# A next chunk's first matmuls issued two steps ahead, and one small copy moved from GpSimd to VectorE

## The chip, the core and the metric

The kernel runs on one core of a Trainium2 chip. The metric is the time of one execution on the device in microseconds (us), lower is better. The engines are called by their short names: PE (TensorE, matmuls), DVE (VectorE), ACT (ScalarE), POOL (GpSimd) and SP (SyncE, which here only issues DMAs). Each engine works through its own instructions in order; ACT, POOL and SP also issue DMAs from their queues.

## The reference

The input x has 2048 rows and 1024 columns (S and D), the hidden width F is 3584. Cut to what matters:

```python
xn = layernorm(x)                                  # over the 1024 columns
X  = rfft2(xn) * (w_r + 1j * w_i)                  # 2048 x 513
s  = irfft2(X, s=(2048, 1024))
h  = silu(xn @ w1)                                 # 2048 x 3584
g  = silu(h @ w2)                                  # 2048 x 1024
return x + s * g
```

So there are two branches on the same normalised input: a two-dimensional Fourier filter, and a feed-forward block. All is float32 in and out.

## The kernel before, in words

Every float32 matmul operand is split into a high and a low float16 part, and each product is made of three passes (high by high, high by low, low by high). The split of a weight is one ACT instruction (the high part, a function `high`, L257) and one DVE instruction (the low part, `low`, L260).

The rows are cut into four chunks c = 0 to 3 of 512 rows, each of four tiles p of 128 rows. `xnT[c]` holds a chunk's normalised input, transposed and split.

PE's stream is a row of groups of the feed-forward block, with the pieces of the Fourier branch set in between:

- First layer, `pa(c,f)` (L466): 24 matmuls of 512 columns for chunk c and the f-th of 28 slices of 128 hidden columns. ACT evacuates a group with silu into `h`; four PSUM buffers (tag "ff") are shared by these groups and a few small sums. After four groups DVE and ACT form sums and differences of h (`hr`, `hosum`, `hoone`), split them, and SP stores them (the `hd` tensors).
- Second layer, `pb(m,j)` (L549 to L551): seven products m, Strassen's way, of eight blocks j. Its weights are loaded by SP as `jr`, for the products m = 4 and 5 joined with a second block by an accumulating DMA that POOL issues (L424), and split by ACT and DVE into `w`. DVE adds the results up in `kept` and `pl`.

The Fourier branch has three stages, each a Python generator that emits its instructions step by step:

- Forward, `fd_gen(c)`: for each tile p the transform over d by 24 matmuls of 128 columns (`fa_mat`, PE L803 to L805, tile `fa(c,p)`), evacuated by two ACT instructions (`fa_evac`, L812 and L813) into `L0`, of which there are two buffers. DVE then does butterflies over each tile (`bfly`), writing `V`. After the four tiles, four steps j = 0 to 3 do a radix-4 step on DVE over the tiles, split the result (`Rs`, ACT L884 and L886, DVE L889 and L890), and SP stores it (`vd`, `vs`).
- Filter, `f_gen`: sixteen tiles `fx(u)`, matmuls over the rows with loaded constants `kq` and the stored `vq`, then on DVE butterflies, the multiplication with w (loaded as `wq`), butterflies back, a split `zq` and a store `zd`. The values at column 512 go another way, through small tensors `zp` and `zps`.
- Inverse, `i_gen(c)`, in the order c = 1, 3, 0, 2: `load_i` loads `zt` from `zd`, `edge_in` copies the column from `zps` (odd c) or `zp` (even c) into `zt` (128 partitions x 16 elements), then four tiles `iu` (PE L1281 for odd c, L1289 for even c), each evacuated by ACT (`uc`) and DVE (`ub`, L1297 and L1298), and four tiles `id` after them.

The tiles `fa`, `fx`, `iu` and `id` all take turns in two PSUM buffers (tag "ft"), so a tile's matmuls wait until the tile two before it has been evacuated.

The order of all this is written by the kernel itself, at build time. After each group of pa or pb a function `work` takes one step of the weight queue, one of an auxiliary queue, and up to three steps of the background queue that holds the Fourier generators. It stops as soon as a modelled DVE clock is more than 1.0 us ahead of a modelled PE clock, or when a step yields PAUSE. The clocks are advanced by every DVE and PE instruction emitted, by a fixed cost and one per element; the numbers that other steps yield play no part. A step can correct the DVE clock by hand, as the four radix-4 steps do with `clock["dve"] -= 0.8`. So how much background work stands between two pa groups follows from these numbers; on the chip the engines then run through their queues in that order, whatever it costs.

In the forward stage, the steps i = 0 to 5 of a chunk issue fa(c,i) in step i, evacuate fa(c,i−1) and do the butterflies of tile i−2. For chunk 0 the matmuls and the first two evacuations are emitted elsewhere, ahead of the generator.

Of the kernel before, what the change touches and what calls it, by code (L numbers as in the profile page):

```python
# [26 lines left out]
IORDER = (1, 3, 0, 2)  # L27
# [105 lines left out]
def spectral_ffn(ctx, tc, x, w_r, w_i, w1, w2, ca, kc, ci, tw, pm, out):  # L133
    nc = tc.nc
# [35 lines left out]
    zps = cp.tile([128, 2, 4, 4, 2], F16, name="zps")  # L170
# [45 lines left out]
    clock = {"pe": 0.0, "dve": 0.0}  # L216
# [16 lines left out]
    def radix4(sign, b, d, o):  # L233

        sub = nc.vector.tensor_tensor
        plus, minus = ((2, 7), (6, 3)) if sign < 0 else ((6, 3), (2, 7))

        def pick(i):
            st = i[1] - i[0]
            stop = i[1] + (1 if st > 0 else -1)  # L240
            return o[:, i[0]:stop:st]

        sw = d[:, 1, ::-1]
        sub(o[:, 0:2], b[:, 0], b[:, 1], op=OP.add)
        sub(o[:, 4:6], b[:, 0], b[:, 1], op=OP.subtract)
        sub(pick(plus), d[:, 0], sw, op=OP.add)
        sub(pick(minus), d[:, 0], sw, op=OP.subtract)
# [551 lines left out]
    def fa_mat(c, p):  # L799
        ps = pt.tile([128, 8, 128], F32, name=f"fa{c}_{p}", tag="ft")  # L800
        sl, xt = slice(p * 128, (p + 1) * 128), xnT[c]
        for d in range(8):
            nc.tensor.matmul(ps[:, d], xt[:, 0, d, sl], A["ca"][:, 0, d], start=True, stop=False)  # L803
            nc.tensor.matmul(ps[:, d], xt[:, 0, d, sl], A["ca"][:, 1, d], start=False, stop=False)
            nc.tensor.matmul(ps[:, d], xt[:, 1, d, sl], A["ca"][:, 0, d], start=False, stop=True)  # L805
        psa[c, p] = ps

    def fa_evac(c, p):
        ps = psa.pop((c, p))
        t0 = A["p"].tile([128, 8, 2, 65], F32, name=f"L0_{c}_{p}", tag="L0", bufs=2)  # L810
        nc.gpsimd.memset(t0[:, :, 1, 0:1], 0.0)
        nc.scalar.activation(t0[:, :, 0], ps[:, :, 0:65], AF.Copy)  # L812
        nc.scalar.activation(t0[:, :, 1, 1:64], ps[:, :, 65:128], AF.Copy)  # L813
        l0[c, p] = t0

    def fd_gen(c):
# [51 lines left out]
            tt(v[:, 1, 0:1], ee[:, 0, 0, 0:1], ee[:, 1, 0, 0:1], op=OP.subtract)  # L868

        for i in range(6):  # L870
            if i < 4 and c:
                fa_mat(c, i)
            if 1 <= i <= 4 and (c or i > 2):
                fa_evac(c, i - 1)
            yield 0
            if i >= 2:
                yield from bfly(i - 2)
            yield 0
        o, sp, total, both = {}, {}, {}, {}

        def high_r(j):
            room = ap.tile([128, 2048 + 256 * len(THREE)], F16, name=f"Rs{c}_{j}", tag="Rs", bufs=2)
            both[j] = room[:, 2048:].rearrange("p (q h k) -> p q h k", h=2, k=128)
            nc.scalar.activation(both[j][:, :, 0], total[j], AF.Copy, scale=2.0**-21)  # L884
            sp[j] = room[:, 0:2048].rearrange("p (q h k) -> p q h k", h=2, k=256)
            nc.scalar.activation(sp[j][:, :, 0], o[j], AF.Copy, scale=2.0**-21)  # L886

        def low_r(j):
            nc.vector.scalar_tensor_tensor(sp[j][:, :, 1], o[j], 2.0**-21, sp[j][:, :, 0], op0=OP.mult, op1=OP.subtract)  # L889
            nc.vector.scalar_tensor_tensor(both[j][:, :, 1], total[j], 2.0**-21, both[j][:, :, 0], op0=OP.mult, op1=OP.subtract)  # L890
            defer(2, lambda: nc.sync.dma_start(vd[j][:, :, c], sp[j]))
            defer(2, lambda: nc.sync.dma_start(vs[j][:, :, c], both[j]))

        for j in range(4):
            sl = slice(128 * j, 128 * j + 128)
            if j:
                high_r(j - 1)
            b = ap.tile([128, 2, 2, 128], F32, name=f"Rb{c}_{j}", tag="Rb", bufs=1)
            d = ap.tile([128, 2, 2, 128], F32, name=f"Rd{c}_{j}", tag="Rd", bufs=1)
            nc.vector.tensor_tensor(b, vt[:, 0:2, :, sl], vt[:, 2:4, :, sl], op=OP.add)  # L900
            nc.vector.tensor_tensor(d, vt[:, 0:2, :, sl], vt[:, 2:4, :, sl], op=OP.subtract)
            if j:
                low_r(j - 1)
            r = ap.tile([128, 8, 128], F32, name=f"Ro{c}_{j}", tag="Ro", bufs=1)
            radix4(-1, b, d, r)
            o[j] = r.rearrange("a (q r) k -> a q (r k)", r=2)
            total[j] = ap.tile([128, len(THREE), 128], F32, name=f"vt{c}_{j}", tag="E", bufs=1)
            some = o[j][:, THREE[0]:THREE[-1] + 1]
            nc.vector.tensor_tensor(total[j], some[:, :, 0:128], some[:, :, 128:256], op=OP.add)
            clock["dve"] -= 0.8  # L910
            yield 3.9
        high_r(3)
        yield 0.5
# [332 lines left out]
    def edge_in(c):  # L1246
        zt = C["z"][c]
        if c % 2:
            zt = zt.rearrange("m (e q h l i) -> m e q h l i", e=2, q=4, h=2, l=8)
            nc.gpsimd.tensor_copy(zt[:, :, :, :, 0, 0], zps[:, :, c])  # L1250
        else:
            zt = zt.rearrange("m (q h r l i) -> m q h r l i", q=4, h=2, r=2, l=8)
            nc.gpsimd.tensor_copy(zt[:, :, :, :, 0, 0], zp[:, c].rearrange("m r q h -> m q h r"))

    def i_gen(c):
        ip = C["p"]
        tt, stt = nc.vector.tensor_tensor, nc.vector.scalar_tensor_tensor
        if c == IORDER[0]:
            edge_in(c)
# [187 lines left out]
        for p in range(5):  # L1447
            if p < 4:
                mat2(p)
            if p:  # L1450
                bfly(p - 1)
            if p == 3 and c != IORDER[-1]:
                edge_in(IORDER[IORDER.index(c) + 1])
            yield 3.4 if p else 0.3
# [41 lines left out]
    with tc.manual_schedule():  # L1496
# [73 lines left out]
        for c in range(4):  # L1570
            add(bg, fd_gen(c))
# [140 lines left out]
```

## Time and profile before

| what | us |
|---|---|
| median of 3 runs (lowest 1228.38, highest 1229.40) | 1229.09 |
| the profiled execution | 1229.27 |
| its span, first to last instruction | 1227.5 |
| PE busy | 1211.4 |
| DVE busy | 1003.7 |
| ACT busy | 496.1 |
| POOL busy | 140.2 |

The granted clock of PE is full (1.00) throughout. By time, the first layer with the forward stage takes the first 635 us, the filter runs from 552 to 839, the second layer from 635 on, the inverse from 879. A row of a timeline reads: start, duration, engine, line, operation, output and input tiles with shapes, count, and in brackets how long the engine had been idle before it and which instruction ended that. A row of the list of waits reads: the waiting engine and its line, the engine it waited for, total us, how many times, the longest.

### The profile page before, as it was taken

Reading aid. Unit: us, or ns where it says so; the run is one execution under the profiler, and the core shown is the slowest. Engines: PE = TensorE matmul, PEld = TensorE weight load, DVE = VectorE, ACT = ScalarE, POOL = GpSimd, SP = SyncE. Lnnn points to the kernel's source line nnn. Section 1 sums busy time; section 2 is a strip of 40 time slices with the busy share of each in tenths; the row PEclk is TensorE's granted clock in tenths of the full one; section 3 lists DMA queues with packets and bytes.
Section 4 is the critical chain, followed back from the end, with each engine's and each line's share of the span. In section 5 each row is a group of like instructions: output and inputs, shape, how many; then the busy total and the mean of one; then the engine's idle time right before and its main releaser. Section 6 shows DMA issues by size and latency. Waiting matters only on the chain.

```text
span 1227.5 us, 19143 instructions
## 1 busy us (share of the span) xinstructions
PE 1211.4 (99%) x6992; PEld 615.1 (50%) x6992; DVE 1003.7 (82%) x2006; ACT 496.1 (40%) x670; POOL 140.2 (11%) x256
## 2 busy tenths in 40 slices
PE   8999999999999999999999999999999999999998
PEld 5544445445444544445445555554445554455545
DVE  7778997898798798958969989995377876997766
ACT  6775553455375654434423222221122322333212
POOL 3320100002010000201101121152111111000000
PEclk9999999999999999999999999999999999999999
DMA  8887585747678978489998999977979999996677
GB/s 251 184 195 188 165 255 180 211 130 214 192 254 276 317 231 270 146 259 208 188 282 279 263 253 233 315 255 221 269 218 302 264 338 310 305 364 244 224 249 274
DMA packets 285055, 299.98 MB, mean 244 GB/s; under 512 B 48928, under 2 KB 211744, under 8 KB 284576
## 3 DMA queue, kind: packets, MB, share of 16 engines
q1 hardware_dynamic: 264944, 239.95, 66.9%
q10 hardware_dynamic: 15840, 50.67, 11.8%
q0 software_dynamic: 4176, 8.13, 3.6%
q8 instruction: 55, 0.90, 0.3%
q14 instruction: 40, 0.33, 0.1%
HBM read 188.05 MB, written 104.35 MB: 238 GB/s over the span
## 4 chain that ended last, share of the span: by engine, by line
PE 59%; DMA 15%; DVE 14%; ACT 3%; issue 3%; SPq 1%; POOL 1%; ACTq 0%; DVEq 0%; POOLq 0%
PE pa L466 33%; PE pb L551 7%; PE pb L549 7%; PE pb L550 7%; DMA jr<-in_B_w_dram 2%; PE id L1371 2%; DMA jr<-ws 1%; DVE Z L1124 1%; DVE w L260 1%; DMA cis<-in_ci_dram 1%; DMA ht<-hd_dif 1%; ACT xp L750 1%; DMA vq<-vd 1%; DMA zd<-zq 1%; DMA zt<-zd 1%
## 5 line engine op out<-in xcount | busy, mean ns | idle before, releaser
L466 PE MATMUL pa<-xnT,w 128*128 128x512 f16 x2688 | 584.3, 379 | 1.3 <-ACT w L257 0.7
L466 PEld LDWEIGHTS <-w 128*128 128x128 f16 x2688 | 261.2, 98 | 312.7 <-issue 1.2
L549 PE MATMUL pb<-w,ht 128*128 128x512 f16 (+2 forms) x812 | 300.4, 372 | 0.0
L550 PE MATMUL pb<-w,ht 128*128 128x512 f16 (+2 forms) x812 | 300.4, 372 | 0.0
L551 PE MATMUL pb<-w,ht 128*128 128x512 f16 (+2 forms) x812 | 300.3, 372 | 0.0
L551 PEld LDWEIGHTS <-ht 128*128 128x128 f16 x812 | 79.4, 98 | 91.1
L549 PEld LDWEIGHTS <-ht 128*128 128x128 f16 x812 | 79.5, 98 | 86.7
L550 PEld LDWEIGHTS <-ht 128*128 128x128 f16 x812 | 79.4, 98 | 86.8
L475 ACT ACTIVATE h<-pa,s 128x512 f32<-128x512 f32 x112 | 75.6, 677 | 77.6 <-PE pa L466 60.2
L257 ACT ACTIVATE w<-jr,sc 128x512 f16<-128x512 f32 x98 | 68.4, 713 | 86.4 <-DMA jr<-in_B_w_dram 45.6
L260 DVE SCALAR_TENSOR_TENSOR w<-jr,sc,w 128x512 f16<-128x512 f32 x98 | 71.3, 743 | 18.8 <-ACT w L257 18.8
L257 ACT ACTIVATE hosum<-hr,hs 128x1536 f16<-128x1536 f32 x28 | 44.0, 1573 | 87.5 <-DVE hr L505 34.9
L260 DVE SCALAR_TENSOR_TENSOR hoone<-h,hs,hoone 128x2048 f16<-128x2048 f32 x28 | 65.6, 2342 | 7.2 <-ACT hoone L257 7.2
L257 ACT ACTIVATE hoone<-h,hs 128x2048 f16<-128x2048 f32 x28 | 55.9, 1995 | 28.6 <-issue 11.1
L504 DVE TENSOR_TENSOR hr<-h 128x1024 f32<-128x1024 f32 x28 | 34.1, 1219 | 21.8 <-ACT h L475 21.8
L260 DVE SCALAR_TENSOR_TENSOR hosum<-hr,hs,hosum 128x1536 f16<-128x1536 f32 x28 | 50.7, 1810 | 1.4 <-ACT hosum L257 1.4
L257 ACT ACTIVATE w<-w1r,rs 128x1024 f16<-128x1024 f32 x28 | 31.9, 1143 | 37.7 <-DVE w L260 24.2
L642 ACT ACTIVATE pl<-pl,c 128x512 f32<-128x512 f32 (+2 forms) x28 | 17.7, 656 | 70.2 <-DVE pl L618 43.6
L424 POOL DMA_DIRECT2D jr<-in_B_w_dram x28 | 24.6, 999 | 180.3 <-DMA jr<-in_B_w_dram 89.7
L1124 POOL TENSOR_TENSOR Z<-yb 128x32 f32<-128x32 f32 x32 | 16.2, 525 | 209.0 <-DVE yb L1103 202.2
L1033 ACT ACTIVATE zq<-Z,zs 128x1024 f16<-128x1024 f32 x16 | 18.4, 1148 | 52.5 <-DVE Z L1124 25.6
L260 DVE SCALAR_TENSOR_TENSOR w<-w1r,rs,w 128x1024 f16<-128x1024 f32 x28 | 35.6, 1273 | 2.3 <-ACT w L257 2.2
(239 smaller groups left out, 1571.6 us busy)
## 6 DMA issues: line engine op xcount, KB each, us to landing
w1r<-in_B_w_dram SPq DMA_DIRECT2D x28, 512.0 KB, 6.6
hd_sum<-hosum SPq DMA_DIRECT2D x56, 256.0 KB, 2.9
hd_one<-hoone SPq DMA_DIRECT2D x56, 256.0 KB, 4.0
hd_dif<-hoone SPq DMA_DIRECT2D x56, 256.0 KB, 4.3
w2m<-in_B_w_dram SPq DMA_DIRECT2D x28, 512.0 KB, 5.6
ht<-hd_dif ACTq DMA_DIRECT2D x32, 448.0 KB, 9.2
jr<-in_B_w_dram SPq DMA_DIRECT2D x56, 256.0 KB, 6.7
ht<-hd_sum ACTq DMA_DIRECT2D x32, 448.0 KB, 5.7
```

What stands on the lines that cost most here:

```text
L257: nc.scalar.activation(hi, raw, AF.Copy, scale=scale)
L260: nc.vector.scalar_tensor_tensor(lo, raw, scale, hi, op0=OP.mult, op1=OP.subtract)
L424: nc.gpsimd.dma_start(raw[n], w2_block(*todo[n], 1), accum_op=OP.add)
L466: nc.tensor.matmul(ps, w[:, wh, d], xt[:, xh, d], start=(n == 0), stop=(n == 23))
L475: nc.scalar.activation(hq[:, 2 * (c % 2) + f % 2], ps, AF.Silu, scale=s1[:, f:f + 1])
L504: tt(sums[:, 0:2], hq[:, 0::2], hq[:, 1::2], op=OP.subtract)
L549: nc.tensor.matmul(ps, hh[:, 0], w[:, 0], start=first, stop=False)
L550: nc.tensor.matmul(ps, hh[:, 0], w[:, 1], start=False, stop=False)
L551: nc.tensor.matmul(ps, hh[:, 1], w[:, 0], start=False, stop=last)
L1033: nc.scalar.activation(zqs[q][:, 0, :, 16 * j:16 * j + 16], zs_[u], AF.Copy, scale=zs)
L1124: eng.tensor_tensor(Z[:, ns, pos], x0[:, :, ls], x1[:, :, ls], op=o_)
L1371: nc.tensor.matmul(ps[:, g, cols], us[g][:, uh, 4 * r + p], C["ci"][:, ch, g, r, cols], start=(r == 0 and n == 0), stop=(r == 1 and n == 2 ...
```

## The change

It has three parts.

First, the matmuls of a chunk's first two tiles in the transform over d, fa(c,0) and fa(c,1), and the evacuation of fa(c,0), are emitted in the radix-4 steps j = 2 and 3 of the chunk before. Within the chunk, step i = 0 issues fa(c,2) and evacuates fa(c,1), step i = 3 issues fa(c,3) and evacuates fa(c,2), step i = 4 evacuates fa(c,3). So each tile's matmuls come two steps ahead of its butterflies. Chunk 0 stays as it was.

Second, the hand correction of the modelled DVE clock in a radix-4 step is 0.5 instead of 0.8.

Third, the copy into zt for the inverse's first chunk (c = 1) is a DVE instruction; for the three others it stays on POOL.

```diff
         for i in range(6):
-            if i < 4 and c:
-                fa_mat(c, i)
-            if 1 <= i <= 4 and (c or i > 2):
-                fa_evac(c, i - 1)
+            if i in (0, 3) and c:
+                fa_mat(c, 2 + i // 3)
+            if i in (0, 3, 4) and (c or i):
+                fa_evac(c, max(i, 2) - 1)
             yield 0
...
         for j in range(4):
+            if j > 1 and c < 3:
+                fa_mat(c + 1, j - 2)
+                if j > 2:
+                    fa_evac(c + 1, 0)
...
-            clock["dve"] -= 0.8
+            clock["dve"] -= 0.5
             yield 3.9
...
         if c % 2:
             zt = zt.rearrange("m (e q h l i) -> m e q h l i", e=2, q=4, h=2, l=8)
-            nc.gpsimd.tensor_copy(zt[:, :, :, :, 0, 0], zps[:, :, c])
+            (nc.vector if c == IORDER[0] else nc.gpsimd).tensor_copy(zt[:, :, :, :, 0, 0], zps[:, :, c])
```

From here on lines of the changed kernel stand four higher than the same lines before, from L900 on. Three places show what moves. Tile names in these rows carry chunk and number, then a running number that means nothing.

ACT around the evacuations of fa(3,0) and fa(3,1), before (`h32` is h, `w2m` a running maximum over w2, `w1` a weight split):

```order
L475 ACTIVATE h32_8_1_4109<-pa2_17_4081,s1_229 128x512
L257 ACTIVATE w1_21_4185<-w1r21_3823,rs1_228 128x1024
L390 ACTIVATE junk_248,w2m_232<-w2m14_3977 128x1024
L812 ACTIVATE L0_3_0_4219<-fa3_0_4126 128x8x65
L813 ACTIVATE L0_3_0_4219<-fa3_0_4126 128x8x63
L475 ACTIVATE h32_8_1_4109<-pa3_16_4151,s1_229 128x512
L390 ACTIVATE junk_248,w2m_232<-w2m15_4016 128x1024
L812 ACTIVATE L0_3_1_4292<-fa3_1_4194 128x8x65
L813 ACTIVATE L0_3_1_4292<-fa3_1_4194 128x8x63
```

Here the evacuation of fa(3,0) stands behind a weight split. The same engine now:

```order
L475 ACTIVATE h32_8_0_3916<-pa0_17_3888,s1_229 128x512
L390 ACTIVATE junk_248,w2m_232<-w2m11_3841 128x1024
L812 ACTIVATE L0_3_0_4032<-fa3_0_3927 128x8x65
L813 ACTIVATE L0_3_0_4032<-fa3_0_3927 128x8x63
L884 ACTIVATE Rs2_2_4036<-vt2_2_3966 128x2x128
L886 ACTIVATE Rs2_2_4036<-Ro2_2_3961 128x4x256
L475 ACTIVATE h32_8_0_3916<-pa1_16_3968,s1_229 128x512
L390 ACTIVATE junk_248,w2m_232<-w2m12_3883 128x1024
L884 ACTIVATE Rs2_3_4093<-vt2_3_4050 128x2x128
L886 ACTIVATE Rs2_3_4093<-Ro2_3_4045 128x4x256
L475 ACTIVATE h32_8_0_3916<-pa1_17_4052,s1_229 128x512
L812 ACTIVATE L0_3_1_4168<-fa3_1_4007 128x8x65
```

The two evacuations come four and three pa groups earlier, among the last steps of chunk 2 (Rs2). On PE the sequence of whole groups was pa(2,17), fa(3,0), pa(3,16), fa(3,1), pa(3,17), fa(3,2), and is now pa(0,17), fa(3,0), pa(1,16), fa(3,1), pa(1,17), pa(2,16), fa(3,2).

The copy into zt for chunk 1, before, on POOL (`jr` are second-layer weights, the DMA rows their joins):

```order
L424 DMA jr56_8644<-in_B_w2_dram 128x512
L424 DMA jr57_8675<-in_B_w2_dram 128x512
L424 DMA jr58_8701<-in_B_w2_dram 128x512
L1250 COPY zt1_8581<-zps_220 128x16
L424 DMA jr59_8733<-in_B_w2_dram 128x512
```

Here the copy stands behind the joins jr56 to jr58. DVE around the same place now:

```order
L598 TENSOR_TENSOR kept5_7103<-kept5_7103,pb2_5_8652 128x512
L260 SCALAR_TENSOR_TENSOR w2_3_1_8544<-jr54_8572,sc2_234,w2_3_1_8544 128x512
L260 SCALAR_TENSOR_TENSOR w2_3_1_8544<-jr55_8619,sc2_234,w2_3_1_8544 128x512
L1254 COPY zt1_8581<-zps_220 128x16
L598 TENSOR_TENSOR kept6_7180<-kept6_7180,pb2_6_8710 128x512
L1301 TENSOR_TENSOR ub1_0_8840<-iu1_0_8788,uc1_0_8838 128x512
```

It leaves the queue of the joins and stands between the split of jr55 and the addition of pb(2,6). The other rows of DVE around it are in the order they had.

SP around the last store of the forward stage (`vd3`, `vs3`) and the first load of the filter (`vq0`), before:

```order
L498 DMA hd_one_0_1_99<-hoone_0_10_1_5226 512x1x256
L498 DMA hd_dif_1_1_91<-hoone_0_10_1_5226 512x1x256
L498 DMA hd_dif_0_1_93<-hoone_0_10_1_5226 512x1x256
L498 DMA hd_one_3_1_97<-hoone_0_10_1_5226 512x1x256
L891 DMA vd3_78<-Rs3_3_5233 512x1x512
L892 DMA vs3_82<-Rs3_3_5233 256x1x256
L966 DMA vq0_5356<-vd0_75 128x2048
```

Here vd3 and vs3 stand behind the four stores of hoone. SP at the same place now:

```order
L891 DMA vd3_78<-Rs3_3_5235 512x1x512
L892 DMA vs3_82<-Rs3_3_5235 256x1x256
L498 DMA hd_one_0_1_99<-hoone_0_10_1_5226 512x1x256
L498 DMA hd_dif_1_1_91<-hoone_0_10_1_5226 512x1x256
L498 DMA hd_dif_0_1_93<-hoone_0_10_1_5226 512x1x256
L498 DMA hd_one_3_1_97<-hoone_0_10_1_5226 512x1x256
L970 DMA vq0_5321<-vd0_75 128x2048
```

The two stores of the forward stage pass the four stores of hoone. The loads vq0 and kq0 wait for vs3 to land, before and now. On PE the first filter tile fx0 stood after pa(0,27) and stands after pa(0,26); from the sixth filter tile on, and through the inverse, PE's order is what it was.

## The prediction

> **What bounds the kernel now.** I read the page's busy times, then the waits of PE, then the timelines of the engines around the two waits that the change touches, and last the windows of DMA share.
>
> ```profile
> span 1227.5 us, 19143 instructions
> PE 1211.4 (99%) x6992; PEld 615.1 (50%) x6992; DVE 1003.7 (82%) x2006; ACT 496.1 (40%) x670; POOL 140.2 (11%) x256
> ```
>
> PE is busy for all but 16.1 us of the span, and the change takes no matmul away, so it can only win what PE waits. These are PE's waits, without those of the first 20 us:
>
> ```profile
> PE iu L1281 <- POOL zt L1250: 2.6, 1, 2.6
> PE iu L1289 <- DVE ub L1298: 1.8, 1, 1.8
> PE fa L803 <- ACT L L813: 1.3, 1, 1.3
> ...
> PE pa L466 <- DMA xnT<-xs: 0.6, 1, 0.6
> ```
>
> Each is one single wait. The change aims at the first (the copy into the inverse's first tile) and the third (a tile of the transform over d). It does not touch the code of the other two.
>
> **The wait of fa.** PE around it, then ACT:
>
> ```profile
> 407.90 5.34 PE L466 MATMUL pa<-xnT,w 128*128 128x512 f16 x24
> 414.58 0.22 PE L803 MATMUL fa<-cas,xnT 128*128 128x128 f16 x1 [1.34 <-ACT L L813]
> ```
>
> ```profile
> 411.37 1.15 ACT L257 ACTIVATE w<-w1r,rs 128x1024 f16<-128x1024 f32 x1 [2.14 <-DVE w L260]
> 412.43 1.04 ACT L390 ACTIVATE junk<-w2m 128x1024 fp8e4<-128x1024 f32 x1
> ...
> 413.95 0.58 ACT L813 ACTIVATE L<-fa 128x504 f32<-128x504 f32 x1
> ```
>
> This is fa(3,2): two PSUM buffers are shared by the fa tiles, so it needs the evacuation of fa(3,0), and that evacuation stands in ACT's queue behind a weight split, which itself waited for DVE until 411.37. Between fa(3,0) and fa(3,2) stand two groups of 24 pa matmuls. In the new order there are three (pa of (1,16), (1,17) and (2,16)), each worth the row below, and the evacuation stands right behind the h of pa(0,17), ahead of the splits of Rs.
>
> ```profile
> 189.99 5.18 PE pa L466 x24
> ```
>
> So the evacuation gets 5.18 us more against a lateness of 1.34: this term is −1.34 us; it begins to shrink only if ACT were 3.84 us later there than now, and is gone at 5.18. For chunks 1 and 2 the same tiles have three groups or more, and no wait stands there today. The 48 matmuls and two evacuations moved per chunk for chunks 1 to 3 keep their number and size, so on PE they cost 0. On ACT an evacuation now comes up to four groups earlier; what could suffer is the evacuation of a pa tile behind it, but four pa buffers give three groups (15.5 us), and the list of PE's waits holds no pa that waited for an evacuation. I take 0, with −1.34 and +1.34 as the ends for a wait of the same size that goes or comes elsewhere. The constant 0.8 that becomes 0.5 adds no instruction; it lets the planner hand out less background work per matmul group: 0 by itself.
>
> **The copy into the inverse's first tile.** PE, POOL, DVE and ACT around it:
>
> ```profile
> 876.73 0.38 PE L551 MATMUL pb<-w,ht 128*128 128x512 f16 x1
> 879.72 2.85 PE L1281 MATMUL iu<-kk,zt 128*128 128x128 f16 x48 [2.61 <-POOL zt L1250]
> ```
>
> ```profile
> 876.66 2.74 POOL L424 DMA_DIRECT2D jr<-in_B_w_dram  x3 [41.31 <-DMA jr<-in_B_w_dram]
> 878.41 1.26 POOL L1250 COPY zt<-zps 128x16 f16<-128x16 f16 x1
> ```
>
> ```profile
> 876.12 0.75 DVE L260 SCALAR_TENSOR_TENSOR w<-jr,sc,w 128x512 f16<-128x512 f32 x1 [11.22 <-ACT w L257]
> 876.79 0.68 DVE L598 TENSOR_TENSOR kept<-kept,pb 128x512 f32<-128x512 f32 x1
> 881.90 0.69 DVE L1297 TENSOR_TENSOR ub<-iu,uc 128x512 f32<-128x512 f32 x1 [4.43 <-ACT uc L1295]
> ```
>
> On POOL the copy stands behind three DMA issues (the joins of jr56 to jr58) that wait for loads, and it takes 1.26 us. On DVE it stands behind the split of jr55 and ahead of kept, so it can start where kept started, at 876.79. No row shows this copy on DVE. The nearest is a DVE instruction of 32 elements:
>
> ```profile
> L1209 DVE SCALAR_TENSOR_TENSOR zp<-edge,zs,zp 128x32 f16<-128x32 f32 x1 | 0.3, 251 | 0.0
> ```
>
> With 0.25 us it ends at 877.04. The iu matmul followed the POOL copy's end (878.41 + 1.26 = 879.67) by 0.05, so now it starts at 877.09 instead of 879.72: −2.63 us. The best end is that PE goes on without a break: the pb matmuls start 0.216 us apart (5.18 / 24), the next one was due at 876.95, so −2.77. The other end within this mechanism is a DVE copy as long as half of POOL's, 0.63: −2.25. I take 2.63, by the row of the same engine. What the copy costs DVE is hidden: DVE idles 4.43 us until 881.90, and if that idleness were gone the price is 0.25. POOL loses an instruction and issues its next join earlier.
>
> A condition is hidden here. The new gate is the landing of jr55 (ACT's split of it, then DVE's at 876.12), and PE now arrives 1.34 us sooner because of fa. If the landing does not move with PE, the 1.34 comes back as a wait. I expect that it moves, since DVE catches up with PE in between and waits for PE's own product:
>
> ```profile
> 636.05 1.22 DVE L504 TENSOR_TENSOR hr<-h 128x1024 f32<-128x1024 f32 x1 [6.80 <-ACT h L475]
> 646.54 2.35 DVE L260 SCALAR_TENSOR_TENSOR hoone<-h,hs,hoone 128x2048 f16<-128x2048 f32 x1 [5.06 <-ACT hoone L257]
> 649.47 0.68 DVE L1099 TENSOR_TENSOR T<-T,T 128x512 f32<-128x512 f32 x1
> ```
>
> Everything from here to 877 hangs on PE's place at 636. Besides, in the new order the four instructions from 649.47 on (two L1099/L1100, two L1103/L1104) stand ahead of the wait at 636.05, where DVE idles anyway, which leaves the chain after 646.54 some room.
>
> **The sum.** −1.34 − 2.63 = −3.97, against the profiled execution's 1229.27 us: 1225.30. The median of the runs lies 0.18 below the profiled execution, inside their spread of 1.0, so I leave 1225.3. From no change a measurement can tell about 0.2%, which is 2.46 us.
>
> **A rule against it.** The row is POOL's: its DMA issue at 876.66 starts 0.13 us before the copy can start on DVE. As a mechanism of this kernel: if POOL's issue holds a way into memory that the copy needs, the copy waits for the end of that issue. One issue of the three is 0.91 us (2.74 / 3), so 877.57, iu at 877.87, and the gain is 1.85 instead of 2.63: 1226.1. If it waits for all three, 879.40, iu at 879.70, and nothing is left of the gain: 1227.9. The split at 876.12 and kept at 876.79 ran beside the same issue at 0.75 and 0.68 us, their usual lengths, which speaks against it, but neither is a copy. The Trainium skill, "SBUF — State Buffer", section "Who interferes with whom", states such a lock: VectorE's copies can take a mode that uses the port pair shared with GpSimd, and whoever starts first keeps it for the whole instruction. By that rule the sum would be one of these two; no run here shows it yet.
>
> **Rivals.**
>
> *The gain is given back at 1038.* PE's second wait is at the inverse's third chunk, behind a joined load. For it speaks how full the DMA engines are before it:
>
> ```profile
> 891.00:905.00 14.00, 14.00 (x85) 7.07 (x83) 13.86 (x38) 4.90 (x7) 1.75 (x2) 1.00 0.57 158
> 966.00:982.00 16.00, 16.00 (x93) 7.98 (x92) 15.30 (x44) 6.23 (x9) 0.86 (x1) 1.00 0.78 238
> 982.00:1024.00 42.00, 42.00 (x264) 22.27 (x263) 34.76 (x85) 11.23 (x24) 4.58 (x6) 1.00 1.02 342
> ```
>
> (The last two numbers of a row are the mean DMA share and GB/s.) If the transfers cannot come sooner, the 2.63 becomes waiting there: 1229.27 − 1.34 = 1227.9. Against it: the shares 0.57 and 0.78 leave 14 × 0.43 + 16 × 0.22 = 9.5 us of free transfer time, so the queue is empty in between, and the chain into that wait begins with DVE waiting for PE again:
>
> ```profile
> 994.29 0.68 DVE L1384 TENSOR_TENSOR sk<-id,sc 128x504 f32<-128x504 f32 x1 [6.72 <-ACT sk L1382]
> ```
>
> *The 1.34 comes back at 877* (the condition above): 1229.27 − 2.63 = 1226.6.
>
> *Slower: the filter's first matmuls overtake their loads.* The new pacing puts the first two filter tiles (fx0, fx1) one group of pa earlier. PE's two starts, POOL's issue of kq0, and SP's rows around the store that both loads wait for:
>
> ```profile
> 552.01 0.27 PE L1001 MATMUL fx<-vq,kq 128*128 128x256 f16 x1
> 559.84 0.27 PE L1001 MATMUL fx<-vq,kq 128*128 128x256 f16 x1
> 536.30 0.86 POOL L960 DMA_DIRECT2D kq<-in_kc_dram  x1 [6.84 <-ACT hoone L257]
> 525.77 1.18 SPq L498 DMA_DIRECT2D hd_one<-hoone  x1
> 530.28 0.98 SPq L892 DMA_DIRECT2D vs<-Rs  x1
> 549.18 0.70 SPq L966 DMA_DIRECT2D vq<-vd  x1
> ```
>
> fx0 would be due at 552.01 − 5.18 − 1.34 = 545.49. Its kq0 took this long, and the two rows below it give the shortest, median and longest landing of all kq and of all vq:
>
> ```profile
> kq<-in_kc_dram POOLq DMA_DIRECT2D x1, 768.0 KB, 9.2
> ...
> DMA to landing us min/median/max: 7.2/8.7/12.9
> ...
> DMA to landing us min/median/max: 3.7/7.0/10.4
> ```
>
> If kq0 is issued no sooner, it lands at 545.5 as now, just in time, or with 12.9 at 549.2: a wait of 3.7. fx1 is then due at 559.84 − 5.18 − 1.34 + 3.71 = 557.03, and its vq1, issued at 549.18 and landing 10.4 later, costs 2.55 more. Together 6.3; from 6.43 on (3.97 + 2.46) the kernel counts as slower, which a tenth more on each load gives: 1231.8. Against it: in the new order of SP the store vs3 stands ahead of the four stores that begin at 525.77, so it is issued 530.28 − 525.77 = 4.5 us sooner, and both loads follow it. That is nearly the whole group.
>
> **How the numbers follow.** Both waits go and nothing takes their place: 0.61, at 1225.3, between 1223.5 (the wait of 1.8 at 1038 goes too) and 1226.6. The 1.34 comes back: 0.08, at 1226.6, half of it counted as faster. Given back at 1038: 0.13, no change. The lock: 0.07, of which 0.04 at 1226.1 and 0.03 at 1227.9. Loads overtaken: 0.11, slower. So faster 0.61 + 0.04 + 0.04 = 0.69, same 0.04 + 0.13 + 0.03 = 0.20, slower 0.11. The range runs from 1223.4 to 1228.2, which takes in all but the slower rival and a few hundredths below.
>
> **What would show it.** After the change PE's waits should have no fa, and no iu at L1285 (the old L1281) above 0.3 us; the copy should be a DVE row of some 0.25 us between the split of jr55 and kept; the wait on ub should still be about 1.8, and fx0 should start near 545.5 without a wait. The prediction is wrong if fx0 or fx1 waits for vq or kq, if the wait on ub grows past 3 us, or if the copy's row starts after 877.5 by the same clock less 1.34.

## The result and the profile after

The changed kernel takes 1234.87 us (median of 12 runs, 1230.92 to 1239.82), the kernel before 1229.59 (12 runs, 1225.93 to 1234.16). The ratio is 1.0046, 95% interval 1.0032 to 1.0060: slower, where 1225.3 and faster was forecast. The profiled execution of the changed kernel took 1231.28 us, so it is one of its quickest.

The page of the changed kernel, and its list of PE's waits (without those of the first 20 us):

```profile
span 1229.5 us, 19142 instructions
PE 1213.2 (99%) x6992; PEld 615.8 (50%) x6992; DVE 1003.3 (82%) x2007; ACT 496.0 (40%) x670; POOL 127.6 (10%) x255
...
PE pa L466 <- ACT h L475: 4.1, 2, 3.2
PE iu L1293 <- DVE ub L1302: 1.5, 1, 1.5
PE pa L466 <- DMA xnT<-xs: 0.5, 1, 0.5
PE eps L1165 <- POOL edge L1158: 0.3, 1, 0.3
```

Both waits that the change aims at are gone: no fa, no iu at L1285. In their place pa waits for the evacuation of an earlier pa, once 3.2 and once 0.95 us, together 4.15 where 3.95 was won. And PE is busy 1.8 us longer (1213.2 against 1211.4) with the same matmuls. That accounts for the profiled execution: 1229.27 − 3.95 + 4.15 + 1.8 = 1231.27, and 1231.28 was measured. The windows of PE around the longer wait show where (the number after the count is the granted clock):

```profile
402.00:404.00 2.00, 1.91 (x9) 1.00 1.04 383
404.00:406.00 2.00, 0.00 (x0) 1.00 1.10 360
406.00:408.00 2.00, 0.89 (x4) 0.89 1.01 307
408.00:410.00 2.00, 2.00 (x6) 0.50 1.07 153
410.00:412.00 2.00, 2.00 (x8) 0.75 0.94 355
412.00:414.00 2.00, 2.00 (x11) 1.00 1.08 389
```

After the stop the clock is halved. The three windows lack 0.11, 0.50 and 0.25 of 2 us, together 1.7 us of full clock, so the halving lasts 3.4 us. It costs those 1.7 us beside the stop itself. The stop of 2.61 in the kernel before had full clock behind it:

```profile
878.00:880.00 2.00, 0.28 (x5) 1.00 0.88 298
880.00:882.00 2.00, 2.00 (x40) 1.00 0.92 176
```

The following rows show where the stop comes from, through DVE, SP and ACT: first three rows of the kernel before (split of hoone(7,0), the loads of w1's slices 20 and 21, ACT's first work on them), then the same of the changed kernel and what follows there:

```profile
366.56 2.35 DVE L260 SCALAR_TENSOR_TENSOR hoone<-h,hs,hoone 128x2048 f16<-128x2048 f32 x1
...
372.09 2.07 SPq L279 DMA_DIRECT2D w1r<-in_B_w_dram  x2
...
377.96 1.06 ACT L283 ACTIVATE junk<-w1r 128x1024 fp8e4<-128x1024 f32 x1 [8.13 <-DMA w1r<-in_B_w_dram]
```

```profile
369.92 0.41 DVE L244 TENSOR_TENSOR Ro<-Rb 128x256 f32<-128x256 f32 x1
...
371.71 2.34 DVE L260 SCALAR_TENSOR_TENSOR hoone<-h,hs,hoone 128x2048 f16<-128x2048 f32 x1
...
376.95 1.70 SPq L279 DMA_DIRECT2D w1r<-in_B_w_dram  x2
...
383.21 1.06 ACT L283 ACTIVATE junk<-w1r 128x1024 fp8e4<-128x1024 f32 x1 [13.70 <-DMA w1r<-in_B_w_dram]
...
399.69 1.53 SPq L892 DMA_DIRECT2D vs<-Rs  x1
...
405.12 0.42 ACT L884 ACTIVATE Rs<-vt 128x256 f16<-128x256 f32 x1 [6.72 <-DMA vs<-Rs]
405.44 1.04 ACT L886 ACTIVATE Rs<-Ro 128x1024 f16<-128x1024 f32 x1
406.39 0.67 ACT L475 ACTIVATE h<-pa,s 128x512 f32<-128x512 f32 x1
```

The new order puts a whole radix-4 step of chunk 2 (Rb, Rd, Ro, vt) on DVE ahead of the low split of hoone(7,0), so that split starts 5.15 us later. The four stores of hoone wait for it at the head of SP's queue, and the loads of w1 stand behind those stores: 372.09 becomes 376.95. ACT, in order, stands for them until 383.21 instead of 377.96, and all its later work, the evacuations of pa among it, comes 5.25 us later. Then ACT meets a second hold: the split of Rs(2,3) needs one of two buffers, and the store of Rs(2,1) was issued only at 399.69, behind three stores of hosum, though DVE had finished it at 392.65. The evacuation of pa(1,17) stands behind that split and ends at 407.06; PE wanted its buffer at 403.91.

### The profile page after: what moved, and what is told of

Its sections match the earlier page's. It is cut to its first block, busy times and chain, and to the rows that moved or that the text cites. A ratio compares the mean times of both kernels' runs of the same rounds, so it can differ in the third digit from the quotient of the medians.

```text
span 1229.5 us, 19142 instructions
## 1 busy us (share of the span) xinstructions
PE 1213.2 (99%) x6992; PEld 615.8 (50%) x6992; DVE 1003.3 (82%) x2007; ACT 496.0 (40%) x670; POOL 127.6 (10%) x255
## 4 chain that ended last, share of the span: by engine, by line
PE 65%; DVE 12%; DMA 10%; ACT 4%; issue 3%; SPq 1%; ACTq 0%; POOL 0%; DVEq 0%; POOLq 0%
PE pa L466 33%; PE pb L550 9%; PE pb L551 9%; PE pb L549 9%; PE id L1375 2%; DMA ht<-hd_dif 2%; DMA zd<-zq 1%; DVE Z L1128 1%; DMA vs<-vs 1%; ACT xp L750 1%; DVE w L260 1%; DMA w1r<-in_B_w_dram 1%; DMA ws<-wd 1%; PE iu L1285 1%; DMA ht<-hd_one 1%
```

## The experiments

Each is compared with the kernel before, run on the same chip. In short:

| kernel | median us | ratio (95%) |
|---|---|---|
| copy alone | 1227.62 | 0.9983 (0.9966 to 0.9999) |
| move alone, 0.8 | 1234.16 | 1.0030 (1.0017 to 1.0042) |
| constant alone | 1228.47 | 0.9992 (0.9976 to 1.0007) |
| move and copy, 0.8 | 1233.47 | 1.0024 (1.0012 to 1.0037) |
| changed, hoone(7,0) stored later | 1231.45 | 1.0019 (0.9998 to 1.0039) |
| changed, Rs(2,1) stored earlier | 1233.68 | 1.0041 (1.0020 to 1.0062) |
| changed, both hoone stored later | 1230.71 | 1.0001 (0.9986 to 1.0017) |
| changed, eps later | 1234.09 | 1.0035 (1.0021 to 1.0048) |
| changed, both hoone and eps later | 1227.16 | 0.9978 (0.9966 to 0.9990) |
| copy and eps later | 1226.44 | 0.9976 (0.9961 to 0.9990) |
| before, one more copy | 1229.58 | 1.0002 (0.9983 to 1.0020) |
| before, fourteen more copies | 1236.10 | 1.0049 (1.0030 to 1.0068) |

**The parts one by one.** Four kernels: the copy alone; the move alone, with the constant at 0.8; the constant alone; move and copy with the constant at 0.8.

The copy alone:

```diff
-            nc.gpsimd.tensor_copy(zt[:, :, :, :, 0, 0], zps[:, :, c])
+            (nc.vector if c == IORDER[0] else nc.gpsimd).tensor_copy(zt[:, :, :, :, 0, 0], zps[:, :, c])
```

> The kernel before with the one small copy on VectorE and nothing else. Theory (the loss sits in the first layer, where the order of chunk 2's radix-4 steps changed): the copy keeps its own gain, so the wait of 2.6 us before the inverse's first tile goes and the time is 1229.3 - 2.6 = 1226.7, ratio 0.998, with the clock at 1.00 as in the profile of before. Rival (the copy on VectorE brings a loss elsewhere in the inverse, or the gain is given back at the next wait): 1229.3 or more, and the wait on ub at 1038 grows from 1.8 to 4.

Measured: 1227.62, ratio 0.9983. The wait at the copy is gone and the wait on ub is 1.6, so the gain is not given back there. The copy on DVE (here with the split of jr55 ahead of it) takes less than thought:

```profile
878.31 0.75 DVE L260 SCALAR_TENSOR_TENSOR w<-jr,sc,w 128x512 f16<-128x512 f32 x1 [10.11 <-ACT w L257]
878.98 0.20 DVE L1250 COPY zt<-zps 128x16 f16<-128x16 f16 x1
```

Of the 2.6 us 2.0 show in the medians; this profile has a halved clock elsewhere (below, eps).

The move alone, as a difference to the changed kernel:

```diff
-            clock["dve"] -= 0.5
+            clock["dve"] -= 0.8
...
-            (nc.vector if c == IORDER[0] else nc.gpsimd).tensor_copy(zt[:, :, :, :, 0, 0], zps[:, :, c])
+            nc.gpsimd.tensor_copy(zt[:, :, :, :, 0, 0], zps[:, :, c])
```

> Only the earlier matmuls of the transform over d, with the constant at 0.8 as before and the copy on GpSimd. In this order the split of hoone for the slices 14 and 15 stands where it stood before, not behind a radix-4 step. Theory (the wait of 3.2 us of pa for its evacuation comes from that split standing 5 us later, ahead of the weight loads on SP): no wait of pa above 1 us, no wait of fa, and the 2.6 at the copy remains: 1229.3 - 1.3 = 1227.9. Rival (the early evacuations alone keep ACT too long, whatever the constant): the wait of about 3 us of pa is there here too, with half clock after it: 1229.3 + 5 - 1.3 = 1233.

Measured: 1234.16, ratio 1.0030. The rival's loss, though not by its wait: no pa waits, but fa does, 4.65 us, with half clock behind it. PE, and ACT at the place:

```profile
391.66 0.22 PE L803 MATMUL fa<-cas,xnT 128*128 128x128 f16 x1 [4.65 <-ACT L L813]
...
384.05 1.06 ACT L283 ACTIVATE junk<-w1r 128x1024 fp8e4<-128x1024 f32 x1 [14.27 <-DMA w1r<-in_B_w_dram]
...
390.54 0.59 ACT L812 ACTIVATE L<-fa 128x520 f32<-128x520 f32 x1
391.03 0.58 ACT L813 ACTIVATE L<-fa 128x504 f32<-128x504 f32 x1
```

The split of hoone(7,0) does stand in its old place among its neighbours, as expected, but one radix-4 step more has come ahead of the whole group, and the loads are as late (issued at 378.28). The early evacuation of fa(3,0) now stands in ACT's queue behind that late load.

The constant alone, as a difference to the kernel before:

```diff
-            clock["dve"] -= 0.8
+            clock["dve"] -= 0.5
```

> Only the constant 0.5 in place of 0.8; matmuls of the transform and the copy as before. The order of the engines is nearly that of before (a few rows of ACT, DVE and SP exchange places). Theory: no new wait, 1229.3 within 0.2%. Rival (the constant by itself makes the loss): a wait of pa of about 3 us and 1234.

Measured: 1228.47, ratio 0.9992: no change that shows, and no new wait. Move and copy with the constant at 0.8, as a difference to the changed kernel:

```diff
-            clock["dve"] -= 0.5
+            clock["dve"] -= 0.8
```

> The changed kernel with the constant back at 0.8: earlier matmuls and the copy on VectorE. Theory (move and copy each keep their gain, the constant together with the move makes the loss): 1229.3 - 1.3 - 2.6 = 1225.4, PE clock 1.00. Rival (the early evacuations make the loss): a wait of pa near 3 us, half clock after it, 1229.3 + 5 - 3.9 = 1230.4 or more.

Measured: 1233.47, ratio 1.0024, with the fa wait of 4.7 again. So the theory that the constant makes the loss together with the move falls. The move makes it, at both values; the constant only decides which matmul waits. The copy wins.

**The chain of the move cut at two places.** First the loads of w1 put ahead of the stores again, in the changed kernel:

```diff
-                    defer(1, lambda k=k, m=m: nc.sync.dma_start(
+                    defer(1 + (n == 4 and (q, g) == (7, 0)), lambda k=k, m=m: nc.sync.dma_start(
```

> The changed kernel, with one thing put back in SP's queue: the four stores of hoone(7,0) come one step later, so the two loads of w1 (slices 20 and 21) stand ahead of them again and needn't wait for the split of hoone, which the new order puts behind a radix-4 step. Theory (these loads are the root: ACT stood 13.7 us for them, and everything behind it on ACT came 5 us late): ACT's wait for w1r falls to 8 us or less, the wait of pa of 3.2 us is gone, PE's clock stays full at 407, and the time is 3.2 + 1.9 below the changed kernel's profiled 1231.3, about 1226. Rival (ACT's lateness does not come from the loads): the wait of pa stays near 3 us and the time at 1231 or more.

Measured: 1231.45, ratio 1.0019. At the place all is as the theory has it: ACT waits 5.98 us for w1r, pa not at all.

```profile
369.06 1.59 SPq L279 DMA_DIRECT2D w1r<-in_B_w_dram  x2
...
375.73 1.06 ACT L283 ACTIVATE junk<-w1r 128x1024 fp8e4<-128x1024 f32 x1 [5.98 <-DMA w1r<-in_B_w_dram]
...
400.81 0.42 ACT L884 ACTIVATE Rs<-vt 128x256 f16<-128x256 f32 x1 [7.69 <-DMA vs<-Rs]
402.08 0.67 ACT L475 ACTIVATE h<-pa,s 128x512 f32<-128x512 f32 x1
```

ACT still stands 7.69 us for the store of Rs(2,1), and it costs nothing now. But PE reaches chunk 3 sooner, and there two waits for evacuations show, of 1.0 (s) and 1.7 (pa), where the changed kernel had one of 0.95. At eps (below) PE waits 0.99 us instead of 0.35, and the clock is halved from 809.9 on, which costs another 1.7. Together these are 4.1 us, nearly all that keeps this profile (1230.55) from the 1226 expected; for the median this was not followed up.

The other cut, at the store of Rs(2,1):

```diff
-            defer(2, lambda: nc.sync.dma_start(vd[j][:, :, c], sp[j]))
-            defer(2, lambda: nc.sync.dma_start(vs[j][:, :, c], both[j]))
+            defer(2 - ((c, j) == (2, 1)), lambda: nc.sync.dma_start(vd[j][:, :, c], sp[j]))
+            defer(2 - ((c, j) == (2, 1)), lambda: nc.sync.dma_start(vs[j][:, :, c], both[j]))
```

> The changed kernel, with the stores of Rs(2,1) one step earlier on SP, ahead of the three stores of hosum instead of behind them. Theory (the second half of the chain: the split of Rs(2,3) on ACT needs the buffer of Rs(2,1), whose store was issued at 398.9, 6.3 us after DVE had finished it): the store is issued near 393, ACT's wait of 6.7 us for it falls to under 2, the evacuation of pa(1,17) ends near 401 where PE needs it at 403.9, no wait of pa, full clock: about 1226 for a run in which no other clock drop happens. Rival (ACT was too late already by the loads of w1): the wait of pa only shrinks and the time stays above 1229.

Measured: 1233.68, ratio 1.0041. The store is issued at 393.64, ACT no longer waits for it, and the stop of pa near 407 is gone; so both halves of the chain are needed for that stop. The time is not better: the same lateness shows at the next place, here with half clock from 529.8 on.

```profile
526.92 0.16 PE L266 MATMUL s<-m1b,unit 128*128 128x2 bf16 x1 [1.95 <-ACT h L475]
528.75 6.59 PE L466 MATMUL pa<-xnT,w 128*128 128x512 f16 x22 [1.67 <-ACT h L475]
```

Near 530 it is the same mechanism in chunk 3: in the changed kernel the low split of hoone(10,0) starts at 508.72 behind a radix-4 step (500.13 before), the loads of slices 26 and 27 are issued at 513.83 (507.28 before), DVE itself waits 5.08 us for them, and ACT then 11.00 us for DVE. So both groups of stores go one step later:

```diff
-                    defer(1, lambda k=k, m=m: nc.sync.dma_start(
+                    defer(1 + (n == 4 and (q, g) in ((7, 0), (10, 0))), lambda k=k, m=m: nc.sync.dma_start(
```

> The same without the change at eps: only the two groups of stores are later. Theory: the waits of 1.0 and 1.7 us near 526, left when only hoone(7,0) was later, go; the spread by the clock drop at eps stays: median 1226 to 1228, best runs 1224. Rival (the waits near 526 have another cause): they stay, median near 1231 as with one group of stores.

Measured: 1230.71, ratio 1.0001: better than the changed kernel, but not the 1226 to 1228 expected. In its profile neither pa nor s waits for ACT any more, and PE begins the inverse at 875.03 without a wait, where the kernel before began it at 879.72:

```profile
875.03 2.84 PE L1285 MATMUL iu<-kk,zt 128*128 128x128 f16 x48
```

Those 4.69 us are more than the 3.97 of the sum. This execution took 1226.34 with one halving of the clock at 1036, the best run 1225.85. Most runs took 1229 to 1233, at mean clocks of 0.994 to 0.997. Most of what they lose lies at the place that comes next: with eps moved as well the median is 3.5 us lower (1227.16, below).

**What else drops the clock.** The copy alone and several others have a second place, the nine small matmuls of eps (the column at 512), which wait for POOL in some executions. In the copy alone:

```profile
806.23 0.40 PE L1161 MATMUL eps<-edge,perm 128*128 128x24 f32 x2 [0.92 <-POOL edge L1154]
...
809.00:810.00 1.00, 1.00 (x5) 0.78 0.96 55
810.00:811.00 1.00, 1.00 (x4) 0.50 0.79 73
```

So eps was put one group of pb later, on top of the copy alone:

```diff
         yield 1
+        yield 1
         ps = pf.tile([128, 512], F32, name="eps", tag="ff")
...
-        yield 1
         b = piece(16).rearrange("m (r q a) -> m r q a", r=2, q=4)
```

> The kernel before with the copy on VectorE, and the nine small matmuls of eps (the column at 512) one group of pb later on PE, with a later pause of the same generator taken out so that its end stays in place. With the copy alone the profile shows a stop of 0.9 us there followed by half clock from 809.8 to 813.1. Theory (part of the spread of all these kernels is this place, in some executions and not in others): no wait at eps, clock 1.00 there, nearly every run at a mean clock of 0.999 or more, median 1.7 us below the copy alone: 1226. Rival (the spread has another source): median 1227.6 as with the copy alone, clocks spread as before.

Measured: 1226.44, ratio 0.9976. No wait at eps, no halving in the profile (PE busy 1211.4), mean clock 1.000 in 8 of 12 runs and 0.998 in the others. It beats both kernels. Then the changed kernel with this alone, and with all three additions:

> The changed kernel with eps one group later and nothing else. It splits the loss of the changed kernel between the first layer and the place at eps. Theory (most of the loss is in the first layer): the wait of pa near 3 us with half clock after it stays, and the drop at eps goes: 1.7 below the changed kernel's 1234.9, about 1233. Rival (most of the slower runs come from eps): 1229 or less.

Measured: 1234.09, ratio 1.0035. The loss stays, so it does not come from eps. In this profile pa waits 3.3 us near 407 and 1.7 near 530, and the inverse's first tile 1.4 for a load (jr).

> The changed kernel with three additions: the stores of hoone(7,0) and of hoone(10,0) one step later on SP, so that the w1 loads of slices 20 and 21 and of 26 and 27 stand ahead of them, and eps one group later on PE. Theory (the earlier matmuls lose by these loads standing behind a split that a radix-4 step delays, in chunk 2 and again in chunk 3, where PE waited 0.95 to 1.7 us near 530): neither pa nor s waits for the evacuation, nothing drops the clock, the gain of fa and of the copy is kept: 1229.3 - 1.3 - 2.6 - 1 = 1224.5, below the 1226.4 of copy and eps alone. Rival (moving radix-4 steps together costs something beyond these loads): waits of pa or s for ACT stay above 1 us in the first layer and the time is above 1226.4.

Measured: 1227.16, ratio 0.9978. From the run before, this one differs in the two groups of stores alone, and it is 6.9 us faster (1234.09 to 1227.16): about that is the price of the chain in the first layer. The loss of the move is undone and eps with it, and the kernel is as fast as copy and eps without the move, no faster. In its profile PE waits 0.7 for an evacuation near 404, 0.57 for jr55 at the inverse's first tile and 2.0 on ub, with half clock behind the latter, where copy and eps alone waited 1.72 and 0.52 at full clock. Whether the 1.3 us of fa are worth anything at all stays open: the two intervals cover one another.

**What a stop costs.** In the kernel before, GpSimd makes the copy once more or fourteen times more (shown); the values are the same:

```diff
             nc.gpsimd.tensor_copy(zt[:, :, :, :, 0, 0], zps[:, :, c])
+            for _ in range(14 if c == IORDER[0] else 0):
+                nc.gpsimd.tensor_copy(zt[:, :, :, :, 0, 0], zps[:, :, c])
```

> The kernel before, in which GpSimd makes the small copy for the inverse's first chunk twice, so PE waits there longer and nothing else changes. It measures what a longer stop of PE costs. Theory (a stop of about 3 us or more, unlike one of 2.6, is followed by half clock for about 3.4 us): wait 2.6 + 1.3 = 3.9, then clock 0.50 for 3.4 us, which costs 1.7 more: 1229.3 + 1.3 + 1.7 = 1232.3. Rival (a stop costs its own length only): 1230.6 and clock 1.00 from 880 to 890.

Measured: 1229.58, ratio 1.0002; it tells nothing. The second copy took 0.25 us, not 1.26, and PE, later by a halving at eps, waited 0.84.

> The kernel before, in which GpSimd makes the small copy for the inverse's first chunk fourteen times more (0.25 us each after the first), 3.5 us in all, so that PE surely stops there for more than 3 us. Theory (a stop of PE of about 3 us or more halves its clock afterwards for about 3.4 us): wait of 3.5 to 6, clock 0.50 for some 3.5 us after about 884, so the time is 1229.3 + 3 + 1.7 = 1234. Rival (a stop costs its own length): full clock after it and about 1232.

Measured: 1236.10, ratio 1.0049. PE waited 7.45 us, 4.84 more than before, and the clock is halved from within the stop on:

```profile
882.00:884.00 2.00, 0.00 (x0) 0.71 1.11 224
884.00:886.00 2.00, 1.13 (x11) 0.50 1.08 196
886.00:888.00 2.00, 2.00 (x22) 0.50 0.74 120
888.00:890.00 2.00, 2.00 (x22) 0.58 1.02 130
```

The halving lasts 6.8 us, some 2 of them within the stop. The first tile's 48 matmuls took 5.12 us instead of 2.85, and PE's busy time is 2.9 longer than before (1214.3 against 1211.4). So a long stop does cost more than its length.

**The changed kernel three times more**, since its one profile shows 1231.3 and its median is 1234.9:

> The changed kernel once more, for a second profile. Theory (the stops near 407 and 530 are each near the length that drops the clock, and the place at eps too): the stop near 407 with half clock is there again, and in an execution at a mean clock of 0.995 to 0.996 one or two more drops of 3.4 us, near 530 or near 810. Rival (the rest is something else, such as longer waits at full clock): one drop only, and a wait that the first profile does not show.

> The changed kernel, a third profile: the stop near 407 with half clock after it, and for each 0.0014 that the mean clock lies under 1 one drop of 3.4 us (3.4 / 2 / 1232), near 407, 530 or 810.

> The changed kernel, a fourth profile: the stop near 407 with half clock after it, and the drops near 530 and near 810 in those executions whose mean clock lies at 0.996 or under; none near 810 where eps does not wait.

Measured: 1234.54, 1235.56 and 1233.27. The stop near 407 is in all three, with half clock behind each:

```profile
PE pa L466 <- ACT h L475: 5.0, 2, 4.0
PE eps L1165 <- POOL edge L1158: 1.9, 1, 1.9
```

```profile
PE pa L466 <- ACT h L475: 3.2, 1, 3.2
PE eps L1165 <- POOL edge L1158: 2.4, 1, 2.4
```

```profile
PE pa L466 <- ACT h L475: 4.9, 2, 4.2
...
PE eps L1165 <- POOL edge L1158: 0.8, 1, 0.8
```

The first two have a halving at eps as well, the third, with a shorter wait there, has not. PE's busy time is 1214.8, 1218.1 and 1214.0 against 1211.4. In the second both halvings last 6.8 us, and PE's 6.7 us more are all of the 6.3 by which it lies over the profile of the kernel before. The mean clocks (0.996, 0.994, 0.999) are within 0.001 of the rule in the expectation (0.997 for two halvings, 0.994 for two of double length, 0.999 for one). So two sources of the 3.6 us between the first profile and the median are seen: longer stops near 407, and halvings at eps that come in some executions. How much each gives to the median is not shown; eps gives little of it, since with eps later the ratio fell only from 1.0046 to 1.0035.

## Why the prediction was wrong

Its steps in order:

- **The wait of fa, −1.34: the wait went, the gain did not.** The failed step is this later sentence of that part: "On ACT an evacuation now comes up to four groups earlier; ... I take 0". It was priced by the evacuations on ACT alone. What the move brings forward with them is a radix-4 step on DVE, and the order of DVE was not followed there to the split of hoone, nor SP's from its stores to the loads of w1 behind them. That chain costs 3.2 + 0.95 us of waits, and 1.7 of clock in the profiled execution. Cutting it at the loads or at the store of Rs takes the stop near 407 away, and putting both groups of stores later is worth 6.9 us of the median.
- **"Four pa buffers give three groups (15.5 us)": mis-sized.** A tile s took one of the four, so the room was 403.91 − 392.02 = 11.9 us, from the end of pa(1,17), which began at 386.84 (and 24 matmuls at 0.216), to the first matmul that needs its buffer. The evacuation ended 15.0 after it.
- **The constant, "0 by itself": right** (0.9992), and not what decides with the move either.
- **The copy, −2.63: right in kind.** The wait is gone wherever the copy is on DVE; it takes 0.20 us, not 0.25, and alone it gives 2.0 of the median. The lock did not happen: in the changed kernel the copy took 0.20 from 880.57 on, with POOL's issue begun at 880.45. The rule of the Trainium skill, "SBUF — State Buffer", section "Who interferes with whom", had no effect at this place. Whether this copy, which writes single elements with gaps between them, takes the mode that the rule is about, no run shows.
- **A stop of PE was priced at its own length.** The prediction took the clock as full throughout. In seven of the eight profiles with a stop of 3.2 us or more half clock followed, which cost some 1.7 to 3 us more.
- **The rivals.** *Given back at 1038*: no, that wait is 1.5 in the changed kernel. *The 1.34 comes back at 877*: not in the first profile of the changed kernel, which comes there later; with copy and eps alone, with the changed kernel and eps, with all three additions and in the last of the four profiles PE does wait 0.6 to 1.7 us for jr55's landing, with both groups of stores later it does not. *The filter's first matmuls overtake their loads*: no, fx0 started at 551.16 without a wait. That is later than the 545.5 of the forecast, by the stops ahead of it; with both groups of stores later it started at 545.10 and did not wait either. So the slower side was held by a mechanism that did not occur, and the one that did was not among the rivals.

## What to carry to other kernels

When a step moves, follow it on every engine's queue to what now stands behind it: here the price lay three queues from the edit, in a weight load behind a store that waits for a split that waits for a moved step. Where a planner decides the order, compare the orders of all engines at the place, not of those that the edit names. And count a stop of PE with the half clock that can follow it; several short ones, well apart, can be cheaper than one of 3 us.

## What the runs showed of the hardware

- **PE's clock halves after stops of about 2 us and more, for 3.4 or 6.8 us, and where the stop falls largely decides whether it does.** Stops with full clock behind them: 2.0 (fa, copy alone), 2.61, 1.0 and 1.7 shortly after one another, and 0.5 to 2.0 on ub in most profiles. With half clock: 3.20, 3.2, 4.0, 4.2, 4.65, 4.7 and 7.45, further 1.95 and 1.67 shortly after one another, and 1.9 and 2.0 on ub in two profiles. Every halving lasted 3.4 or 6.8 us. A stop of 3.26, longer than the 3.20 and at the same place, left the clock full (the changed kernel with eps later):

```profile
404.00:406.00 2.00, 0.00 (x0) 1.00 1.09 360
406.00:408.00 2.00, 0.81 (x4) 1.00 1.02 303
408.00:410.00 2.00, 2.00 (x11) 1.00 1.04 175
```

- **The clock changes on a grid.** In every profile all its drops and rises up to the last matmul, and the drop after it, lie whole multiples of 3.413 us apart: in the changed kernel 407.56 and 1226.76 (240 intervals), in its second profile 407.48 and 813.66 (119), in its third 405.74 and 811.92 (119). The grid lies elsewhere in each execution, and that is the part of chance. PE's busy time in windows cut along the grid tells the two outcomes apart (at full clock, from 25 us to the last matmul, eps aside): every interval in which PE stood still for 2.02 us or more was followed by half clock (nine of them, from 2.02 to 3.41), none with 1.82 or less was; between lie one that was (1.91) and three that were not (1.91, 1.92, 2.01). Of the 3.20 us 2.96 fell into one interval, the 3.26 were divided into 1.82 and 1.44.
- The Trainium skill, "TensorE: Matmul & The Clock Gate", section "What's actually happening", tells of a free-running window of about 3.4 us and half clock after an idle one. The grid and the lengths of the halvings agree with it; but an interval need not be idle throughout, some 2 us of standstill were enough here. At eps even less was: in the copy alone the interval before the drop (806.14 to 809.56) holds 0.18 us of standstill and the whole of the eps matmuls, 2.3 us with 8 and 24 columns each, so this small work counted there for little more than none.
- **The same small copy took 0.25 to 1.27 us on GpSimd:** 1.22 to 1.27 behind the joins ahead of the inverse's first tile (five kernels), 0.25 right after that one (one more copy), 4.35 for fourteen in a row. The cause was not sought.
